# Rebuilding 64-bit weights with a parametric ReLU in an attention and MLP kernel on one core

## The chip, the core and the metric

The kernel runs on one core of a Trainium2 chip. The metric is the device time of one execution in microseconds (us), as the median of several runs. A core has five instruction streams that run side by side and wait for each other through semaphores: TensorE (PE, matrix products into PSUM), VectorE (DVE), ScalarE (ACT), GpSimd (POOL), and SyncE (SP), which here only issues DMA transfers.

## What is computed

```python
q_pool = q.reshape(B, H, S // 2, 2, D).mean(axis=3)         # B, H, S, D = 4, 8, 1152, 64
scores = 1 / sqrt(D) * q_pool @ k.transpose(0, 1, 3, 2)
attn = softmax(scores)
x = (attn @ v), heads side by side                          # 2304 x 512
h = x @ w_in                                                # 512 x 2048
out = (h * sigmoid(h)) @ w_out                              # 2048 x 512, result 2304 x 512
```

The two weight matrices arrive as 64-bit floating point numbers. No engine computes in that format, so the kernel builds the 32-bit number from the two 32-bit words of each weight by integer operations.

## The kernel before

**Attention.** Two heads make a pair, 16 pairs in all, four per batch. A job is one pair and 128 pooled queries; the last 64 queries of two pairs share a job. That gives 18 jobs per batch, 72 in all, numbered from 0. A job computes its scores on PE into the PSUM tiles S0 and S1 (L708), the row maxima on DVE (`TENSOR_REDUCE`, L765), and the exponentials with their sums on ACT (L781, tile p). Each p is split into an fp16 high part (a cast, L398 on ACT or L402 on DVE) and an fp16 remainder (L422, on POOL or DVE), both in the tile phl. Two DMA transposes on SP's queue (L808) turn phl into pt. PE multiplies pt with V (L916, tile po), and DVE divides by the sums (L988, tile x). There is one set of score tiles, so the scores of a job wait for the exponentials of the job before. In the first four jobs one side is transposed by PE (pp, L822) in place of the DMA.

**MLP.** When a batch's four pairs have finished 128 queries, those 512 numbers per row are a block. 18 blocks follow, each of 192 products with w_in (L1111), tanh on ACT (L1125), the gate on DVE (L1132), a split into two fp16 parts (g), and 48 products with w_out (L1206; the last block L1159). PE mixes the blocks' products with the jobs.

**Weights.** `weights(n)` (L540) prepares one of 32 pieces of 128x512 numbers. A transfer brings 128x1024 words into a tile named wide (the first 16 pieces) or raw (the last 16). Then, for each piece:

1. L398 on ACT or L404 on DVE: t = high word, read as fp32, times 2^-111, into a PSUM tile (named mm).
2. L600 on ACT: the top three bits of the low word, in place.
3. L611 on DVE: (t << 3) | low bits. The shift moves exponent and mantissa into their fp32 place and pushes the sign bit out.
4. L619 on DVE: (high word & 0x80000000) | t, which puts the sign back.
5. For w_in alone: a scaling in place (L398).
6. The fp16 high part (L398, ACT) and the fp16 remainder (L422, POOL).

**The order of the work.** `Plan.order` walks through all operations by a priority number and by estimated costs of each engine, and writes one fixed order of instructions per engine. Priorities come from `PRI` (L59) plus the job's number, and from `MLP_EVAC` and `T_EVAC` (L75). An operation with several engines (`either`, L385) goes to the engine that would end it first. With `early=True` DVE is taken off that list. The pools of tiles bound how far the order runs ahead.

Of the kernel before, what the change touches and what calls it, by code (L numbers as in the profile page):

```python
# [27 lines left out]
F32 = mybir.dt.float32  # L28
# [8 lines left out]
P = 128  # L37
# [16 lines left out]
WAIT = 0.206  # L54
PREP_LEAD = 2.029
FIRST_LEAD, FIRST_STEP = -1.602, 3.771
W_FIRST, W_STEP, W2_LATER = 3.378, 0.358, -0.109
V_LATER = 613.5
PRI = dict(  # L59
    score=-3861.412,  # L60
    top=-11.405,
    exp=0.634,
    hi=1.998,
    lo=0.473,
    turn=4.325,
    flip=60509.245,
    flat=-3.873,
    sums=-1535.234,
    rows=-1498.338,
    side=-1.092,  # L70
    load=-8.662,
    raw=0.151,
    xturn=-36.995,
)
EARLY, KL_EARLY, T_EARLY, WLO_EARLY, ADD_EARLY = 8, 2, False, True, True  # L75
MLP_EVAC, T_EVAC = 9.35, -2973.437
# [9 lines left out]
MODE_SWITCH, COLD, COLD_FACTOR = 0.096, 38.0, 2.0  # L86
# [11 lines left out]
EARLY_BY = "act", "dve"  # L98
W_BY = "act", "dve"
# [6 lines left out]
AHEAD, SWITCH, STEAL = 2.802, 386.698, 1.299  # L106
# [18 lines left out]
class Op:  # L125
# [5 lines left out]
    def __init__(self, options, priority, tiles, port, moves, matmuls, mode):  # L131
        self.options, self.priority, self.tiles, self.port = options, priority, tiles, port
        self.moves, self.matmuls, self.mode = moves, matmuls, mode
        self.after, self.before, self.missing = [], [], 0
        self.at = self.start = self.end = None
# [6 lines left out]
class Plan:  # L142
# [7 lines left out]
    def add(self, options, priority, reads=(), writes=(), tiles=(), port=True, moves=None, matmuls=0, mode=0):  # L150
        tiles = [x for t in tiles for x in (t, t.share) if x is not None]
        op = Op(options, priority, tiles, port, moves, matmuls, mode)
# [26 lines left out]
    def order(self):  # L179
# [39 lines left out]

        def pick(e, now):  # L220
            for item in waiting[e]:
                op = item[2]
                if op.at[e] > now + WAIT or not has_room(op):
                    continue
# [23 lines left out]
        while len(order) < len(self.ops):  # L248
# [11 lines left out]
            while moved:  # L260
                moved = False
                for e in engines:
                    if free[e] > now + 1e-9:
                        continue
                    item = pick(e, now)
# [11 lines left out]
                    if e == "pe":  # L277
                        if now < COLD:
                            cost *= COLD_FACTOR
                        if op.mode != mode:  # L280
                            cost += MODE_SWITCH
                        mode = op.mode
# [33 lines left out]
                    order.append(op)  # L316
                    for a in op.after:
# [27 lines left out]
def tile_kernel(tc, q, k, v, w_in, w_out, out):  # L345
    nc = tc.nc
    with ExitStack() as ctx:
# [37 lines left out]
        def either(options, *args, early=False, **kw):  # L385

            if early:  # L390
                options = [o for o in options if o[0] != "dve"] or options
# [909 lines left out]
```

## Time and profile before

| | us |
|---|---|
| median of 3 runs | 723.63 (722.24 to 724.0) |
| the profiled execution's own time | 726.18 |
| its span, from the first to the last instruction | 724.4 |

The span is read as two stretches. In the first 160 us the loads arrive, the weights are rebuilt and the first jobs run. After that, blocks and jobs alternate on PE until only MLP products are left (the last 65 us). The profile has, for each engine, busy times in any stretch; a group's row gives the busy time, the mean duration in nanoseconds and the idle time just before the group's instructions with what ended it; a timeline's row gives start, length, engine, line and operation.

### The profile page before, as it was taken

How to read it: one execution, taken by the hardware profiler on the slowest of the kernel's cores; microseconds unless marked ns; L12 is line 12 of the kernel's file. 1: busy time of each engine (PE TensorE's matmuls, PEld its weight loads, DVE VectorE, ACT ScalarE, POOL GpSimd, SP SyncE). 2: the span in 40 equal slices, each digit the busy share in tenths (PEclk: the TensorE clock that was granted, in tenths of full speed). 3: DMA queues.
4: the chain of work that ended last, by engine and by line, in shares of the span. 5: the costliest groups of instructions: out<-in, count | busy, mean ns of one | idle time of the engine just before them, and what ended most of it. 6: DMA issues, size and time to landing. Idle time of an engine off the chain costs nothing.

```text
span 724.4 us, 23311 instructions
## 1 busy us (share of the span) xinstructions
PE 652.5 (90%) x10052; PEld 470.8 (65%) x10052; DVE 472.4 (65%) x852; ACT 495.6 (68%) x722; POOL 470.7 (65%) x264
## 2 busy tenths in 40 slices
PE   4544877979899999998999999999999999999997
PEld 2333555656758685857585858585758585858767
DVE  3888987977867765775875656477697565754110
ACT  4998897897658676775766767675766675765221
POOL 3536886888657676667647877868547676767111
PEclk8798899999999999999999999999999999999999
DMA  8999889999999999999999999999999998999000
GB/s 345 334 306 216 131 158 226 232 193 206 204 320 189 191 164 179 175 224 184 238 208 198 161 185 165 173 243 191 242 208 182 172 176 160 165 166 161 24 15 16
DMA packets 362888, 138.11 MB, mean 191 GB/s; under 512 B 350112, under 2 KB 350368, under 8 KB 362784
## 3 DMA queue, kind: packets, MB, share of 16 engines
q1 hardware_dynamic: 362624, 136.49, 100.0%
q8 instruction: 78, 1.28, 0.7%
q14 instruction: 26, 0.21, 0.1%
q10 hardware_dynamic: 160, 0.13, 0.1%
HBM read 45.09 MB, written 4.72 MB: 69 GB/s over the span
## 4 chain that ended last, share of the span: by engine, by line
PE 57%; DMA 12%; POOL 9%; DVE 8%; ACT 6%; issue 6%; SPq 1%; POOLq 0%; ACTq 0%; DVEq 0%
PE mm L1111 18%; PE mm L1206 17%; PE S L708 11%; PE po L916 10%; DMA pt<-phl 9%; POOL phl L422 4%; DVE nm L765 4%; POOL w L422 2%; ACT p L781 2%; DMA ld<-v 2%; POOL g L422 2%; ACT phl L398 2%; PE mm L1159 1%; SPq L808 1%; DVE mm L611 1%
## 5 line engine op out<-in xcount | busy, mean ns | idle before, releaser
L422 POOL TENSOR_TENSOR phl<-p,phl 128x1152 f16<-128x1152 f32 x121 | 292.6, 2424 | 125.4 <-ACT phl L398 71.6
L781 ACT ACTIVATE p<-S,nm 128x1152 f32<-128x1152 f32 x144 | 175.0, 1216 | 97.9 <-DVE nm L772 52.1
L765 DVE TENSOR_REDUCE nm<-S 128x1 f32<-128x1152 f32 x144 | 194.6, 1351 | 53.5 <-PE S L708 53.4
L1111 PE MATMUL mm<-xt,w 128*128 128x128 f16 x3456 | 204.4, 220 | 7.0 <-DVE t L1132 4.3
L1111 PEld LDWEIGHTS <-w 128*128 128x128 f16 x3456 | 196.7, 98 | 12.4 <-issue 7.4
L1206 PE MATMUL mm<-w,g 128*128 128x512 f16 x816 | 186.5, 379 | 2.0 <-DVE t L1132 1.4
L916 PE MATMUL po<-V,pt 128*128 128x64 f16 (+1 forms) x4320 | 132.0, 195 | 24.5 <-DMA pt<-phl 12.7
L708 PE MATMUL S<-K,Q 64*128 64x512 f16 (+7 forms) x1320 | 136.3, 369 | 13.7 <-ACT p L781 7.3
L916 PEld LDWEIGHTS <-pt 128*128 128x128 f16 (+1 forms) x4320 | 123.1, 101 | 37.9 <-DMA pt<-phl 16.0
L422 POOL TENSOR_TENSOR g<-t,g 128x512 f16<-128x512 f32 x72 | 96.1, 1337 | 69.6 <-ACT g L398 67.9
L398 ACT ACTIVATE phl<-p 128x1152 f16<-128x1152 f32 x115 | 132.2, 1160 | 9.1 <-DMA pt<-phl 5.9
L1206 PEld LDWEIGHTS <-g 128*128 128x128 f16 x816 | 75.8, 98 | 86.1 <-issue 2.6
L1132 DVE SCALAR_TENSOR_TENSOR t<-t,mm 128x512 f32<-128x512 f32 x72 | 49.4, 686 | 68.8 <-ACT t L1125 68.1
L708 PEld LDWEIGHTS <-Q 64*128 64x128 f16 (+1 forms) x1080 | 42.0, 96 | 50.1 <-issue 9.3
L398 ACT ACTIVATE g<-t 128x512 f16<-128x512 f32 x72 | 45.2, 627 | 21.9 <-DVE t L1132 21.6
L1125 ACT ACTIVATE t<-mm 128x512 f32<-128x512 f32 x72 | 42.5, 590 | 25.4 <-PE mm L1111 25.1
L743 DVE TENSOR_SCALAR r<-sum 128x1 f32<-128x1 f32 (+1 forms) x152 | 17.2, 148 | 52.2 <-ACT p L781 51.7
L708 PEld LDWEIGHTS S<-K,Q 64*128 64x128 f32 (+1 forms) x240 | 22.3, 204 | 39.5 <-issue 22.9
L988 DVE TENSOR_TENSOR x<-po,r 128x128 f32<-128x128 f32 x72 | 20.7, 287 | 21.0 <-PE po L916 18.6
L422 POOL TENSOR_TENSOR xs<-x,xs 128x512 f16<-128x512 f32 (+1 forms) x18 | 22.5, 1248 | 16.6 <-ACT xs L398 16.5
L422 DVE TENSOR_TENSOR phl<-p,phl 128x1152 f16<-128x1152 f32 x19 | 28.3, 1495 | 5.8 <-ACT phl L398 4.9
L525 DVE SCALAR_TENSOR_TENSOR V<-ld,V 128x1152 f16<-128x1152 f32 x16 | 21.9, 1373 | 13.5 <-ACT V L398 13.4
(53 smaller groups left out, 415.2 us busy)
## 6 DMA issues: line engine op xcount, KB each, us to landing
ld<-q SPq DMA_DIRECT2D x16, 576.0 KB, 5.2
ld<-v SPq DMA_DIRECT2D x16, 576.0 KB, 6.1
ld<-k SPq DMA_DIRECT2D x12, 576.0 KB, 6.6
pt<-phl SPq DMA_TRANSPOSE x280, 4.4
wide<-w_in SPq DMA_DIRECT2D x8, 512.0 KB, 7.3
wide<-w_out SPq DMA_DIRECT2D x8, 512.0 KB, 8.1
raw<-w_in SPq DMA_DIRECT2D x8, 512.0 KB, 5.8
raw<-w_out SPq DMA_DIRECT2D x8, 512.0 KB, 5.4
```

The lines of the kernel that those rows point to most:

```text
L398: nc.scalar.activation(out=out(), in_=src(), func=AF.Copy, scale=scale or 1.0)
L422: return lambda: getattr(engine, op)(out=out(), in0=a(), in1=b())
L525: lambda: nc.vector.scalar_tensor_tensor(out=values(1), in0=v3(), scalar=V_SCALE, in1=values(0)[:, :, :D], op0=ALU.mult, op1=ALU.subtract,),
L708: nc.tensor.matmul(o[to, c], lhsT=a[rows, s], rhs=x[rows, c], start=n == 0, stop=n == len(terms) - 1,)
L765: lambda: nc.vector.tensor_reduce(out=nm(), in_=ps()[:, :S], op=ALU.max, axis=AX.X),
L781: lambda: nc.scalar.activation(out=p32(), in_=ps()[:, :S], func=AF.Exp, scale=0.0625, bias=nm(), **({} if SUM_BY_PE else dict(accum_out=sm ...
L916: nc.tensor.matmul(o[to, keep : keep + n], lhsT=pt[:, hl * NK + c, cols], rhs=vv[:, at : at + n], start=c == 0 and hl + vl == 0, stop=c == ...
L988: lambda: nc.vector.tensor_tensor(out=to(), in0=sides2()[:, :, :D], in1=r().unsqueeze(2).to_broadcast([P, 2, D]), op=ALU.mult,),
L1111: nc.tensor.matmul(o, lhsT=w[:, f // 2 % 4, wl, cols], rhs=moving(xl, kk), start=kk == 0 and wl + xl == 0, stop=kk == 3 and wl == 1,)
L1125: lambda: nc.scalar.activation(out=t(), in_=h(), func=AF.Tanh, scale=1.0 / G_SCALE),
L1132: lambda: nc.vector.scalar_tensor_tensor(out=t(), in0=t(), scalar=1.0, in1=h(), op0=ALU.add, op1=ALU.mult,),
L1206: nc.tensor.matmul(o(), lhsT=g[ff // 4]()[:, gl, ff % 4], rhs=w[:, u % 4, wl, e * DM : e * DM + DM], start=ff == ffs[0] and gl + wl == 0, ...
```

## The change

- Steps 1 and 4 of a weight become one. `Prelu` on ACT multiplies by 2^-111, and negative numbers by -(2^32) in addition. A negative weight so leaves step 1 positive, with an exponent larger by 32, which is one bit; the shift by three moves that bit to the sign's place. Step 3 then writes the finished number straight into the tile wide or raw, and L619 is gone. Step 1 can no longer go to DVE.
- Step 2 may go to DVE as a logical shift to the right by 29, step 5 to ACT, DVE or POOL, step 6's cast to ACT, DVE or POOL.
- The flag `early` is gone: in the first jobs the casts and remainders of p, q, k, v and the weights may go to DVE.
- All priorities are new numbers, the first 8 jobs get additions of their own (`PRE`, `SOON`), the weights' steps too (`W`), and the MLP's operations have one number each (`EV`). The planner's notion of when PE's products cost double is a different one. `SPARE` is 0, so no filler product is made.
- The correction of the sums (`guard`) is one instruction with two constants in place of one; the second constant is 1.

```diff
-MLP_EVAC, T_EVAC = 9.35, -2973.437
+PRE = dict(
+    score=-0.266, top=0.223, exp=2.744, hi=1.295, lo=-1.698, turn=-0.57, sums=1.5, side=-0.268,
+)
+W = dict(
+    t=0.374, low=0.166, put=-3777.77, more=0.289, hi=0.49, lo=-0.918,
+)
...
-W_BY = "act", "dve"
+W_BY = "act", "dve", "pool"
+MORE_BY = "act", "dve", "pool"
+LOW_BY = "act", "dve"
...
-            if early:
-                options = [o for o in options if o[0] != "dve"] or options
...
-            either(
-                cast(512, t, value, 2.0**-111, fast=False),
-                pr, [("raw", *tok)], [("t", *tok)], [t, raw], port=False, early=T_EARLY,
-            )
+            add(
+                "act", act_cost(512, True) + 0.06,
+                lambda: nc.scalar.activation(
+                    out=t(), in_=value(), func=AF.Prelu, scale=2.0**-111, alpha=-(2.0**32)
+                ),
+                pr + W["t"], [("raw", *tok)], [("t", *tok)], [t, raw], port=False,
+            )
...
+            def low_on(engine):
+                return lambda: engine.tensor_scalar(
+                    out=words(0).bitcast(U32), in0=words(0).bitcast(U32), scalar1=29, scalar2=None,
+                    op0=ALU.logical_shift_right,
+                )
...
             add(
                 "dve", slow,
                 lambda: nc.vector.scalar_tensor_tensor(
-                    out=tu(), in0=tu(), scalar=3, in1=words(0).bitcast(U32),
+                    out=words(1).bitcast(U32), in0=tu(), scalar=3, in1=words(0).bitcast(U32),
                     op0=ALU.logical_shift_left, op1=ALU.bitwise_or,
                 ),
-                T_EVAC, [("low", *tok)], [("t", *tok)], [t, raw], port=False,
-            )
-            add(
-                "dve", slow,
-                lambda: nc.vector.scalar_tensor_tensor(
-                    out=words(1).bitcast(U32), in0=words(1).bitcast(U32), scalar=0x80000000,
-                    in1=tu(), op0=ALU.bitwise_and, op1=ALU.bitwise_or,
-                ),
-                T_EVAC, [("t", *tok)], [("raw", *tok)], [t, raw], port=False,
+                pr + W["put"], [("low", *tok), ("t", *tok)], [("raw", *tok)], [t, raw], port=False,
             )
```

**The order on DVE at the start.** S are the scores of job 0, V the split values, ld a loaded tile. Before:

```order
L525 SCALAR_TENSOR_TENSOR V_117<-ld_91,V_117 128x1152
L765 TENSOR_REDUCE nm_126<-S_14_110 128x1
L772 TENSOR_SCALAR nm_126<-nm_126 128x1
L765 TENSOR_REDUCE nm_133<-S_13_109 128x1
L772 TENSOR_SCALAR nm_133<-nm_133 128x1
L525 SCALAR_TENSOR_TENSOR V_128<-ld_97,V_128 128x1152
```

Now (line numbers shift by 10 to 19):

```order
L432 TENSOR_TENSOR Q_103<-ld_87 128x576
L535 SCALAR_TENSOR_TENSOR V_117<-ld_91,V_117 128x1152
L432 TENSOR_TENSOR Q_122<-ld_93 128x576
L784 TENSOR_REDUCE nm_125<-S_14_110 128x1
L791 TENSOR_SCALAR nm_125<-nm_125 128x1
L784 TENSOR_REDUCE nm_132<-S_13_109 128x1
L791 TENSOR_SCALAR nm_132<-nm_132 128x1
L535 SCALAR_TENSOR_TENSOR V_127<-ld_97,V_127 128x1152
```

The additions that pool q for jobs 0 and 1 came from POOL to DVE, and the second of them stands ahead of job 0's maxima.

**The order on ACT at the first weights.** wide_107 holds the first four pieces, mm is the PSUM tile t, pt and pp belong to job 0. Before:

```order
L398 ACTIVATE mm_178<-wide_107 128x512
L600 ACTIVATE wide_107<-wide_107 128x512
L398 ACTIVATE mm_184<-wide_107 128x512
L600 ACTIVATE wide_107<-wide_107 128x512 x2
L398 ACTIVATE wide_107<-wide_107 128x512
L672 ACTIVATE pt_157<-pp_191 128x128
L398 ACTIVATE w_0_39_197<-wide_107 128x512
```

Now (L606 is the Prelu, L613 the low bits):

```order
L613 ACTIVATE wide_107<-wide_107 128x512
L606 ACTIVATE mm_180<-wide_107 128x512
L613 ACTIVATE wide_107<-wide_107 128x512
L606 ACTIVATE mm_184<-wide_107 128x512
L408 ACTIVATE wide_107<-wide_107 128x512
L408 ACTIVATE w_0_37_191<-wide_107 128x512
```

The two pieces follow each other with the same kinds of steps; L619 between the merge and the scaling is what is missing on DVE.

**The order on SP at the loads of pair 3.** ld and K are the loads of q, k and v, wide those of weights. Before:

```order
L585 DMA wide_107<-w_in 128x1024 x2
L585 DMA wide_107<-w_out 128x1024
L464 DMA ld_124<-q 128x1152
L464 DMA K_130<-k 128x1152
L464 DMA ld_140<-v 128x1152
```

Now:

```order
L595 DMA wide_107<-w_in 128x1024 x2
L595 DMA wide_107<-w_out 128x1024 x2
L595 DMA wide_129<-w_in 128x1024 x2
L595 DMA wide_129<-w_out 128x1024
L827 DMA_TRANSPOSE pt_175<-phl_161 128x9x128 x2
L474 DMA ld_201<-q 128x1152
L474 DMA K_204<-k 128x1152
L474 DMA ld_215<-v 128x1152
```

The loads of pair 3 moved behind four more loads of weights and behind the first two transposes.

## Rows read from the trace of the kernel before

**Rows 1.** The page: the span

```profile
span 724.4 us, 23311 instructions
```

**Rows 2.** Windows: length, PE, PEld, DVE, ACT, POOL busy us, then PEclk, DMA, GB/s

```profile
0.00:160.00 160.00, 105.48 (x1292) 72.20 (x1292) 125.84 (x228) 133.24 (x206) 106.06 (x71) 0.90 1.00 240
20.00:80.00 60.00, 32.65 (x368) 21.70 (x365) 51.09 (x92) 55.85 (x92) 31.69 (x22) 0.83 1.00 265
80.00:160.00 80.00, 63.63 (x898) 45.39 (x897) 67.42 (x126) 68.42 (x104) 65.50 (x41) 0.98 1.02 193
160.00:724.00 564.00, 546.99 (x8764) 398.61 (x8761) 346.59 (x625) 362.41 (x517) 364.67 (x194) 1.00 1.01 177
```

**Rows 3.** Timeline of PE: start, length; scores of jobs 0, 3, 8 and 18

```profile
6.10 4.21 PE L708 MATMUL S<-K,Q 64*128 64x512 f32 x12 [6.10 <-POOL Q L422]
...
40.34 2.21 PE L708 MATMUL S<-K,Q 64*128 64x512 f32 x12 [0.27 <-issue]
...
92.71 2.21 PE L708 MATMUL S<-K,Q 64*128 64x512 f32 x12 [1.46 <-ACT p L781]
...
183.71 1.64 PE L708 MATMUL S<-K,Q 64*128 64x512 f16 x18
```

**Rows 4.** Waits of PE from 160 us on: total us, times, longest

```profile
PE po L916 <- DMA pt<-phl: 11.2, 13, 2.1
```

**Rows 5.** Timeline of ACT: steps from one start to the next

```profile
67.42 1.15 ACT L398 ACTIVATE phl<-p 128x1152 f16<-128x1152 f32 x1
68.47 0.65 ACT L600 ACTIVATE wide<-wide 128x512 int32<-128x512 uint16 x1
...
70.77 1.21 ACT L600 ACTIVATE wide<-wide 128x512 int32<-128x512 uint16 x2
71.87 1.21 ACT L781 ACTIVATE p<-S,nm 128x1152 f32<-128x1152 f32 x1
```

**Rows 6.** Groups by form: the weights' operations | busy, mean ns | idle before

```profile
L619 DVE SCALAR_TENSOR_TENSOR wide<-wide,mm 128x512 uint32<-128x512 uint32 x16 | 11.0, 689 | 0.7
L611 DVE SCALAR_TENSOR_TENSOR mm<-mm,wide 128x512 uint32<-128x512 uint32 x16 | 11.1, 697 | 2.8 <-ACT wide L600 1.4 <-ACT mm L398 0.9
L404 DVE TENSOR_SCALAR mm<-wide 128x512 f32<-128x512 f32 x9 | 6.2, 686 | 0.1
L398 ACT ACTIVATE mm<-wide 128x512 f32<-128x512 f32 x7 | 4.4, 627 | 0.9 <-DMA wide<-w_in 0.9
L600 ACT ACTIVATE wide<-wide 128x512 int32<-128x512 uint16 x16 | 10.4, 666 | 0.5 <-DMA wide<-w_in 0.5
```

**Rows 7.** Timeline of DVE: the first job, and the step of the second merge

```profile
9.52 1.36 DVE L525 SCALAR_TENSOR_TENSOR V<-ld,V 128x1152 f16<-128x1152 f32 x1 [9.52 <-ACT V L398]
10.80 1.35 DVE L765 TENSOR_REDUCE nm<-S 128x1 f32<-128x1152 f32 x1
...
65.39 0.69 DVE L619 SCALAR_TENSOR_TENSOR wide<-wide,mm 128x512 uint32<-128x512 uint32 x1
66.00 1.35 DVE L765 TENSOR_REDUCE nm<-S 128x1 f32<-128x1152 f32 x1
```

**Rows 8.** Groups by form: nearest rows to the operations that are new

```profile
L402 DVE CAST phl<-p 128x1152 f16<-128x1152 f32 x25 | 19.7, 789 | 1.6 <-issue 0.9 <-DMA pt<-phl 0.3
L422 DVE TENSOR_TENSOR ld<-ld 128x576 f32<-128x576 f32 x9 | 10.7, 1192 | 0.8 <-DMA ld<-q 0.7
L1125 ACT ACTIVATE t<-mm 128x512 f32<-128x512 f32 x72 | 42.5, 590 | 25.4 <-PE mm L1111 25.1
```

**Rows 9.** Timeline of SP's queue, and the page's DMA issues: KB, us to landing

```profile
19.18 9.36 SPq L808 DMA_TRANSPOSE pt<-phl  x2
...
ld<-k SPq DMA_DIRECT2D x12, 576.0 KB, 6.6
```

**Rows 10.** Timeline of POOL: the same addition without and with DVE's V work beside it

```profile
4.60 1.40 POOL L422 TENSOR_TENSOR Q<-ld 128x576 f32<-128x576 f32 x1 [3.23 <-DMA ld<-q]
9.81 2.33 POOL L422 TENSOR_TENSOR Q<-ld 128x576 f32<-128x576 f32 x1 [3.81 <-DMA ld<-q]
```

More of the change, by code (lines that the diff above doesn't have):

```diff
@@ L105 @@
 LAST = B * FULL + B // 2 - 1
-AHEAD, SWITCH, STEAL = 2.802, 386.698, 1.299
 class Tile:
@@ L218, in departs, with windows @@
             return now
+        warm, used, busy, until = False, 0.0, 0.0, WINDOW
+        def windows(now):
+            nonlocal warm, used, until
+            while now >= until:
+                warm = used >= (COOL if warm else HOT) * WINDOW
+                used = min(WINDOW, max(0.0, busy - until))
+                until += WINDOW
         def pick(e, now):
@@ L222, in pick @@
                 op = item[2]
+                if op.spare and warm and used > KEEP * WINDOW:
+                    continue
                 if op.at[e] > now + WAIT or not has_room(op):
@@ L247, in order @@
                 release(op, 0.0)
-        while len(order) < len(self.ops):
+        todo = sum(not op.spare for op in self.ops)
+        while todo:
             if not events:
@@ L277, in order @@
                     if e == "pe":
-                        if now < COLD:
-                            cost *= COLD_FACTOR
+                        if not warm:
+                            cost *= 2.0
                         if op.mode != mode:
                             cost += MODE_SWITCH
-                        mode = op.mode
+                        mode, busy = op.mode, now + cost
+                        used += min(busy, until) - now
                     op.start, op.end = now, now + cost
@@ L533, in prepare @@
                     "pool", 0.1, lambda: nc.gpsimd.memset(values(0)[:, :, D : D + 1], 1.0),
-                    pr + V_LATER, [], [("one", p)], [vt[p]],
+                    pr + (V_FIRST if first else V_LATER), [], [("one", p)], [vt[p]],
                 )
@@ L603, in shift @@
                 )
+            def low_on(engine):
[3 more added lines that the diff above has]
+                )
+            ways = {
+                "act": ("act", act_cost(512) + 0.02, low_act),
+                "dve": ("dve", dve_cost(512, True), low_on(nc.vector)),
+            }
             either(
-                [("act", act_cost(512), shift)],
-                pr, writes=[("low", *tok)], reads=[("raw", *tok)], tiles=[raw], port=False,
+                [ways[x] for x in LOW_BY],
+                pr + W["low"], writes=[("low", *tok)], reads=[("raw", *tok)], tiles=[raw],
             )
@@ L630, in weights @@
                 either(
-                    cast(512, value, value, more, by=W_BY),
-                    pr, writes=[("raw", *tok)], tiles=[raw], early=True,
+                    [(e, c + (0.15 if e == "act" else 0.0), f) for e, c, f in cast(512, value, value, more, by=MORE_BY)],
+                    pr + W["more"], writes=[("raw", *tok)], tiles=[raw],
                 )
@@ L728, in job @@
             add(
-                "pe", cost, lambda: scores(j), j + PRI["score"],
+                "pe", cost, lambda: scores(j), j + pri(j, "score"),
                 inputs, [("S", j, 0), ("S", j, 1)], [*st["S"], *own],
@@ L1127, in first @@
                     ),
-                    MLP_EVAC, [], [tok, ("gt", bid, u)], [h, t], port=False,
+                    EV["tanh"], [], [tok, ("gt", bid, u)], [h, t], port=False,
                 )
@@ L1247, in block, with spin, matmuls @@
             second()
+        def spin(n):
+            ps = tile("psM", "mm", [P, 512], F32, "spin")
+            def matmuls():
+                x = one().bitcast(F16)
+                for _ in range(4):
+                    nc.tensor.matmul(ps()[:, :256], lhsT=x[:, :P], rhs=x, start=True, stop=True)
+            add("pe", 4 * pe_cost(256), matmuls, 1e8 + n, [("one",)], [], [ps, one], matmuls=4, spare=True)
+        for n in range(SPARE):
+            spin(n)
         for p in range(PPB):
```

128 lines of the change are left out of this document (63 added, 65 removed).

## The prediction

> **What bounds the kernel now.** I read the busy times by stretch first, because the kernel has two stages with different limits [rows 2]. From 160 us to the end PE is busy 547.0 of 564 us at the full granted clock: that stage is as long as its products. In the first 160 us PE is busy 105.5 us, so 54.5 us of its 71.5 idle us lie there, and the granted clock is 0.90 on average, 0.83 between 20 and 80 us, a mixture of 1.2 and 2.4 GHz. There ACT is busy 55.9 of 60 us and DVE 51.1, POOL only 31.7. Between 80 and 160 us ACT, DVE and POOL all have 65 to 68 of 80 us. So the start is paced by ACT, with DVE close behind, and whatever shortens ACT's and DVE's work per job in the start moves the whole PE-bound stage forward. The scores show the pace [rows 3]: job 0 at 6.1 us, job 8 at 92.7, job 18 at 183.7.
>
> After 160 us the 17 us of idle PE are mostly waits of the products with V for their transposes, 11.2 us in 13 waits [rows 4].
>
> **What the change does on ACT.** I counted instructions in the two orders up to the same landmark, the exponentials of a job, and priced each by the step from one start to the next, since ACT's instructions overlap a little: 1.05 us for a cast of 1152 columns and 0.55 us for one of 512 [rows 5]. Up to job 8: low bits 22 to 10, -6.6 us; casts of p 12 to 9, -3.2; copies for t 7, now 19 Prelus, +6.6 if a Prelu takes a copy's time; scalings 10 to 8, -1.1; high casts of weights 19 to 15, -2.2; other 512-wide ones five to three, -1.1. Sum -7.6 us. Up to job 12 the same counting gives -11.3 us, up to job 17 -7.9 us, since by then all 32 Prelus stand against 10 copies.
>
> The price of the Prelu is in no row. Its bounds: from below the tanh of 512 columns out of PSUM, 590 ns [rows 8]; from above twice the copy into PSUM, 1254 ns. I take the copy itself, 627 ns [rows 6], since it has the same operands and a tanh costs no more than a copy. The Trainium skill, on the page "ScalarE: Activation LUTs", section "Step-by-step: what each stage is for", states one element per cycle and lane whatever the function. By that the Prelu costs what the copy does, which is the sum above; no row here shows a Prelu. The order has a single load of activation tables, as before, so no switch of tables is added.
>
> **What it does on DVE.** Up to the maxima of job 8 it loses 19 second merges, whose step is 0.61 us [rows 7], and 12 copies of 686 ns [rows 6]: -19.8 us. It gains 11 shifts, three casts of p at 0.79 us and two additions of q at 1.19 us [rows 8], and four operations of 512 columns, for which I take the merge's 0.69 [rows 6]. A shift of 512 columns in place lies between 0.35 us, the cast's rate [rows 8] on fewer columns, and 0.69 us, the rate of the merges; I take 0.40, since like the cast it has one source and lies in SBUF. That adds 4.4 + 2.4 + 2.4 + 2.8 = 12.0 us, or 15.2 with slow shifts. Sum -7.8 us, or -4.6. So both engines that pace the start are relieved by nearly the same amount, and neither hides the other's gain. The merge that stays writes SBUF from PSUM and SBUF, as the removed one did, so I leave it at 0.69 us. The correction of the sums keeps its count and size: nothing. The new maker of filler products is switched off: nothing.
>
> **What it moves.** On DVE the second addition of q stands ahead of job 0's maxima. V's remainder ran 9.52 to 10.88 us and the maxima began at 10.80 [rows 7]; they now wait one addition more, +1.2 us, which the queue behind them (V of pair 1, the sums) and ACT's first exponentials inherit. On SP the loads of pair 3 come behind four more loads of weights and two transposes. Before, those transposes held the queue from 19.2 to 28.5 us [rows 9]; the loads then land some 6 us later [rows 9], near 34 us, while job 3's scores started at 40.3 [rows 3], and would start near 37 now. I cost this at nothing; the cover is about 3 us, and what comes later than that delays job 3 by as much. The transposes of job 0 are queued ahead of them and need POOL's remainder.
>
> **The sum.** What counts is how much PE work is done by when. From the scores of job 56 on PE's order is the same in both. Ahead of job 8's scores the new order has 1.3 us more products (24 L1111 fewer, 12 L1206 more), ahead of job 12's 3.3 us less, ahead of job 18's 4.2 us more. The gain on ACT plus that, less the 1.2 us: 7.7 at job 8, 6.8 at job 12, 7.9 + 4.2 - 1.2 = 10.9 at job 18. PE is saturated between the last two, nearer to the last. I take 9.5 us. In the PE-bound stage I expect no change: DVE, ACT and POOL have 61 to 65% there, and the loads of the later batches stand within one job of where they stood in SP's order. 724.4 us [rows 1] become 714.9. The profiled execution took 726.18 us, 2.6 above the median of 723.63, and its span 0.8 above it; I take the gain from the median: 723.63 - 9.5 = **714.1 us**.
>
> The spread of this case: slow shifts would make DVE the bound and leave 4.6 - 1.2 + 1.3, some 5 us; the end at job 18 gives 11. Scores at the low clock take 4.21 us where warm ones take 2.21 [rows 3]; a job or two more or fewer in that state are 2 to 4 us. The waits for transposes [rows 4] can move by a third, 4 us. Together 707 to 720.
>
> **The rivals.**
> - *The removed work was covered.* POOL and the transposes, not ACT and DVE, would pace the stretch from 80 to 160 us, and the gain up to job 8 is given back there. For it: POOL is busy 65.5 of 80 us there [rows 2]; and the same addition of q took POOL 1.40 us with DVE idle and 2.33 us beside DVE's V work with two SBUF inputs [rows 10, 7]. The change puts 13 shifts and eight more casts of p on DVE up to job 17, 13 x 0.40 + 8 x 0.79 = 11.5 us in which POOL might stand. Against it: POOL has 14.5 idle us there and half of 20 to 80 us. If two thirds of the 11.5 us fell on the path, 1.8 us of gain would be left: 721.8. The Trainium skill, "GPSIMD Engine Reference", "Key points", says that GpSimd shares its SBUF interfaces with VectorE and contends with VectorE's two-port modes or two SBUF inputs. That speaks against this change; the rows on the addition agree for two inputs, and no row here shows it for a one-source operation.
> - *Prelu is dear.* On ACT, behind each Prelu the scalings, casts and exponentials wait. If it goes through the columns twice, each costs 0.43 us more (a cast of 1152 columns takes 0.50 us more than one of 512 [rows 5], 0.78 ns a column, times 512 gives 0.40; the upper bound above gives 0.63; I take 0.43, a little over the first). At 0.43, 32 of them are 13.8 us: 714.1 + 13.8 = 727.9, slower than before. It decides from 9.5 / 32 = 0.30 us on, a Prelu of 0.93 us. Against it: tanh, exponential and copies all keep one rate.
> - *More is gained.* PE, with fewer holes, keeps 2.4 GHz through the start, and the new priorities close half of the waits after 160 us: 9.5 + 3 + 5.6, 705.5 us. For it: clock 0.83 between 20 and 80 us. Against it: the places of the loads and transposes in SP's order hardly moved.
> - *The new order waits more in the middle.* The waits of rows 4 double: 714.1 + 11.2 = 725.3.
>
> **How the numbers follow.** The forecast has 0.62, covered work 0.13, more gain 0.12, the dear Prelu 0.06, more waits 0.07. The range for 8 in 10 takes the forecast's spread and most of the larger gain and of the covered case: 706 to 722. About 0.3%, 2.2 us, is what a measurement of this kernel can tell from no change. Faster by more than that, below 721.4: the forecast, the larger gain and nearly half of the covered case, 0.79. Within it: the rest of the covered case and some of the waits, 0.11. Slower: 0.10.
>
> **What would show it.** Right: job 8's scores near 85 us and job 18's near 176; busy DVE in the first 160 us lower by some 10 us at equal work; Prelus of 0.6 to 0.7 us; PE's idle time from 160 us on about 17 us as before. Shifts near 0.4 us show the DVE price, additions of q ahead of job 0's maxima the 1.2 us. Wrong: Prelus above 0.9 us; POOL over 95% busy from 80 to 150 us, with its remainders longer than now; job 3 waiting for its loads; or waits for transposes well over 11 us.

## The result, and the profile after

| kernel | median us | lowest to highest | runs |
|---|---|---|---|
| before | 723.71 | 722.24 to 724.0 | 4 |
| changed | 715.92 | 714.45 to 718.18 | 4 |
| changed, in the next series | 714.53 | 711.05 to 715.39 | 6 |

The ratio of changed to before is 0.9897, with a 95% interval of 0.9872 to 0.9921: 1.0% faster, 7.8 us by the medians. The second series gave 0.9868 [0.9846, 0.9890] against a median of 722.89 us of the kernel before. The forecast was 714.1 us. The profiled execution of the changed kernel took 714.45 us, the lowest of its four, and that of the kernel before 726.18, above the highest of the table; so their spans differ by more, 11.9 us, than the medians. A second profile of the changed kernel (714.33 us) has job 8's and job 18's scores within 1 us of the first, so what is read below from the pair of traces is some 3 to 4 us more than the medians bear out, and most of that belongs to the one execution of the kernel before.

The page of the changed kernel, its span and PE's line:

```profile
span 712.5 us, 23295 instructions
...
PE 653.3 (92%) x10052; PEld 470.7 (66%) x10052; DVE 471.9 (66%) x839; ACT 480.4 (67%) x707; POOL 463.9 (65%) x260
```

Windows of the changed kernel (busy us with the number of instructions in brackets, then granted clock, DMA share, GB/s). They answer to [rows 2]:

```profile
core 0: us, PE busy (x) PEld busy (x) DVE busy (x) ACT busy (x) POOL busy (x), PEclk, DMA share, GB/s
0.00:160.00 160.00, 116.32 (x1456) 79.47 (x1458) 120.48 (x221) 132.03 (x209) 112.20 (x76) 0.90 1.05 251
20.00:80.00 60.00, 38.88 (x482) 26.71 (x479) 49.56 (x94) 52.21 (x86) 41.94 (x29) 0.82 1.00 270
80.00:160.00 80.00, 67.61 (x948) 47.45 (x949) 59.83 (x113) 69.47 (x111) 65.80 (x40) 0.98 1.11 210
160.00:712.00 552.00, 537.03 (x8600) 391.20 (x8596) 351.46 (x619) 348.36 (x499) 351.65 (x185) 1.00 0.99 178
```

PE's idle time in the first 160 us fell from 54.5 to 43.7 us, and after 160 us from 17.0 to 15.0. So 10.8 of the 12.8 us that PE idles less lie in the start, at an unchanged granted clock of 0.90. DVE and ACT were not busier; they did less for each job. The products themselves took the same time in both, 652.5 us busy before and 653.3 now over the whole span, so all of the gain is idle time of PE.

The scores of jobs 3, 8 and 18 in PE's timeline answer to [rows 3]: 3.5, 8.3 and 5.3 us earlier.

```profile
36.87 2.21 PE L723 MATMUL S<-K,Q 64*128 64x512 f32 x12 [0.27 <-issue]
...
84.41 2.21 PE L723 MATMUL S<-K,Q 64*128 64x512 f32 x12
...
178.43 1.64 PE L723 MATMUL S<-K,Q 64*128 64x512 f16 x18
```

How much work each engine did up to the same scores is read from windows that end where these start. The kernel before, to jobs 8, 12 and 18:

```profile
0.00:92.71 92.71, 50.01 (x533) 33.54 (x533) 70.11 (x125) 73.57 (x116) 49.94 (x36) 0.85 0.97 265
0.00:133.85 133.85, 84.42 (x999) 58.61 (x999) 104.13 (x187) 108.32 (x170) 83.42 (x57) 0.89 0.98 242
0.00:183.71 183.71, 129.19 (x1641) 87.64 (x1642) 143.58 (x260) 152.13 (x232) 124.60 (x81) 0.92 1.02 233
```

The changed kernel, to the same jobs:

```profile
0.00:84.41 84.41, 51.39 (x520) 33.09 (x520) 64.44 (x116) 66.87 (x106) 50.81 (x39) 0.84 0.97 283
0.00:122.48 122.48, 79.53 (x957) 54.06 (x957) 90.94 (x165) 96.60 (x153) 80.12 (x56) 0.89 1.02 261
0.00:178.43 178.43, 134.14 (x1743) 90.94 (x1744) 137.15 (x246) 144.92 (x227) 126.59 (x83) 0.91 1.05 247
```

ACT has 6.7, 11.7 and 7.2 us less to do (predicted 7.6, 11.3 and 7.9), DVE 5.7 us less to job 8 (predicted 7.8). PE's work moved by +1.4, -4.9 and +5.0 us (predicted +1.3, -3.3, +4.2).

The groups of the weights' steps (busy us, mean ns, idle time before) answer to [rows 6]; L606 is the Prelu, L613 and L619 the low bits on ACT and on DVE, L634 the merge that stays:

```profile
L606 ACT ACTIVATE mm<-raw 128x512 f32<-128x512 f32 x16 | 9.9, 626 | 0.3 <-DVE x L1007 0.3
L606 ACT ACTIVATE mm<-wide 128x512 f32<-128x512 f32 x16 | 9.8, 631 | 0.0
L613 ACT ACTIVATE raw<-raw 128x512 int32<-128x512 uint16 x11 | 7.1, 663 | 3.6 <-DMA raw<-w_in 3.6
...
L619 DVE TENSOR_SCALAR raw<-raw 128x512 uint32<-128x512 uint32 x5 | 5.5, 1114 | 0.0
L619 DVE TENSOR_SCALAR wide<-wide 128x512 uint32<-128x512 uint32 x8 | 3.7, 482 | 0.2 <-DMA wide<-w_out 0.2
...
L634 DVE SCALAR_TENSOR_TENSOR wide<-mm,wide 128x512 uint32<-128x512 uint32 x16 | 10.6, 685 | 3.4 <-ACT mm L606 3.4
```

The Prelu costs what the copy did, 627 ns. The shift was expected at 0.40 us; 13 of them took 9.2 us together, 0.71 each, because some of them waited for POOL (the last section has the rows).

### The profile page after: what moved, and what is told of

Its sections match the earlier page's. It is cut to its first block, busy times and chain, and to the rows that moved or that the text cites. A ratio compares the mean times of both kernels' runs of the same rounds, so it can differ in the third digit from the quotient of the medians.

```text
span 712.5 us, 23295 instructions
## 1 busy us (share of the span) xinstructions
PE 653.3 (92%) x10052; PEld 470.7 (66%) x10052; DVE 471.9 (66%) x839; ACT 480.4 (67%) x707; POOL 463.9 (65%) x260
## 5 line engine op out<-in xcount | busy, mean ns | idle before, releaser
L432 POOL TENSOR_TENSOR g<-t,g 128x512 f16<-128x512 f32 x72 | 98.4, 1368 | 80.4 <-ACT g L408 79.6
L723 PE MATMUL S<-K,Q 64*128 64x512 f16 (+7 forms) x1320 | 138.2, 373 | 13.4 <-ACT p L800 6.7
L408 ACT ACTIVATE phl<-p 128x1152 f16<-128x1152 f32 x99 | 114.4, 1160 | 8.2 <-DMA pt<-phl 5.8
L412 DVE CAST phl<-p 128x1152 f16<-128x1152 f32 x41 | 33.7, 822 | 9.9 <-DMA pt<-phl 7.1
L432 POOL TENSOR_TENSOR xs<-x,xs 128x512 f16<-128x512 f32 (+1 forms) x16 | 19.8, 1238 | 24.3 <-ACT xs L408 24.1
L432 DVE TENSOR_TENSOR phl<-p,phl 128x1152 f16<-128x1152 f32 x21 | 32.1, 1533 | 4.4 <-ACT phl L408 4.2
L535 DVE SCALAR_TENSOR_TENSOR V<-ld,V 128x1152 f16<-128x1152 f32 x16 | 27.6, 1729 | 6.6 <-ACT V L408 6.6
```

The source lines that it names most:

```text
L408: nc.scalar.activation(out=out(), in_=src(), func=AF.Copy, scale=scale or 1.0)
L412: nc.vector.tensor_copy(out=out(), in_=src())
L432: return lambda: getattr(engine, op)(out=out(), in0=a(), in1=b())
L535: lambda: nc.vector.scalar_tensor_tensor(out=values(1), in0=v3(), scalar=V_SCALE, in1=values(0)[:, :, :D], op0=ALU.mult, op1=ALU.subtract,),
L723: nc.tensor.matmul(o[to, c], lhsT=a[rows, s], rhs=x[rows, c], start=n == 0, stop=n == len(terms) - 1,)
```

## The experiments

Eleven kernels besides the changed one were run. Two things were kept apart: which operations are issued, and in which order. Where an edit reaches the planner, a new order is written for the whole kernel; "in place" means that the order was kept and only the instruction at its place was exchanged. Each run's ratio is told against the kernel before on the same chip (medians 722.57 to 723.47 us); differences to the changed kernel are taken from its second series, 714.53 us.

The theory: ACT and DVE both pace the start, and the change pays because it takes work from both. The rivals: the work removed was covered; or the order, not the operations, makes the gain.

### The changed kernel again, and one engine's work put back (in place)

The changed kernel without an edit:

> The changed kernel unchanged, timed again beside the others of this call. Both theories: ratio to before 0.987 to 0.992 (714 to 718 us), job 8's scores near 84 us, job 18's near 178 us; a reference for the other runs of this call.

Measured 714.53 us. The second merge put back in place, with a plain copy for the Prelu:

```diff
-                lambda: nc.scalar.activation(
-                    out=t(), in_=value(), func=AF.Prelu, scale=2.0**-111, alpha=-(2.0**32)
-                ),
+                lambda: nc.scalar.activation(out=t(), in_=value(), func=AF.Copy, scale=2.0**-111),
...
+                nc.vector.scalar_tensor_tensor(
+                    out=words(1).bitcast(U32), in0=words(1).bitcast(U32), scalar=0x80000000,
+                    in1=tu(), op0=ALU.bitwise_and, op1=ALU.bitwise_or,
+                )
...
```

> The changed kernel with the second merge put back on DVE right behind the first (32 instructions of 0.69 us, a step of 0.61, 19.5 us in all, 11.6 us up to job 8), t by a plain copy on ACT, every other instruction in the changed kernel's order. Theory (DVE and ACT pace the first 160 us, so a DVE step there costs time): most of the gain is lost, 8 to 13 us slower than the changed kernel, 724 to 729 us. Rival (the removed merge was covered and the gain comes from the new order, priorities and engine choices): within 3 us of the changed kernel, 714 to 719 us.

Measured 726.17 us, ratio 1.0037 [1.0018, 1.0057], 11.6 us above the changed kernel. Each Prelu issued twice in place:

```diff
-                lambda: nc.scalar.activation(
+                lambda: [nc.scalar.activation(
                     out=t(), in_=value(), func=AF.Prelu, scale=2.0**-111, alpha=-(2.0**32)
-                ),
+                ) for _ in range(2)],
```

> The changed kernel with every Prelu issued twice on ACT (32 more instructions at a step of 0.55 us, 17.6 us in all, 10.5 us up to job 8), every other instruction in the same order. Theory (ACT paces the start): 9 to 15 us slower than the changed kernel, 725 to 731 us, job 8's scores near 94 us. Rival (POOL, the transposes or the job's chain of waits pace the start, ACT has room): 0 to 4 us slower, 716 to 720 us.

Measured 722.79 us, 0.9992 [0.9974, 1.0010], 8.3 us above the changed kernel. The first 160 us, with the merge back (first row) and with Prelus doubled (second):

```profile
0.00:160.00 160.00, 109.53 (x1290) 74.32 (x1290) 127.91 (x231) 124.31 (x194) 101.18 (x69) 0.89 0.99 238
```

```profile
0.00:160.00 160.00, 108.91 (x1316) 72.50 (x1316) 110.83 (x207) 142.12 (x227) 103.41 (x71) 0.89 1.00 239
```

Now DVE (127.91 us) or ACT (142.12) is the busiest, the other falls back, and PE gets 109 us of work done in place of 116.32. So neither engine has slack for 32 more instructions: 32 merges at a step of 0.61 us are 19.5 us, of which 11.6 / 19.5 = 0.59 fell on the path; 32 Prelus at 0.55 are 17.6, of which 8.3 / 17.6 = 0.47 did. "Covered work" falls in this order.

These two prices hold more than waiting. The same runs up to job 18's scores, with the merge back (first row) and with Prelus doubled (second), have the same products ahead of them as the changed kernel's window that ends at 178.43:

```profile
0.00:190.08 190.08, 137.97 (x1742) 94.39 (x1743) 154.57 (x278) 148.35 (x227) 125.32 (x83) 0.91 1.01 233
```

```profile
0.00:187.81 187.81, 134.33 (x1744) 90.71 (x1744) 134.26 (x246) 165.45 (x259) 125.57 (x83) 0.91 1.02 237
```

PE idles 52.1 and 53.5 us there against 44.3, that is 7.8 and 9.2 us more; with the merge back it is also busy 3.8 us longer for the same products. That run's granted clock was 0.94 from 80 to 160 us, against 0.98. By idle time alone the merges cost 0.40 us per us and the Prelus 0.52, so which of the two engines is the tighter one is not settled by the two prices.

### The operations alone, in the old order

The first try let the planner write the order. The kernel before, with Prelu and one merge:

```diff
-            either(
-                cast(512, t, value, 2.0**-111, fast=False),
+            add(
+                "act", act_cost(512, True) + 0.06,
+                lambda: nc.scalar.activation(
+                    out=t(), in_=value(), func=AF.Prelu, scale=2.0**-111, alpha=-(2.0**32)
+                ),
...
```

> The kernel before with the Prelu and the single merge alone; old priorities, low bits on ACT alone, casts of the first jobs barred from DVE as before. DVE loses 32 merges and 22 copies, ACT gains 22 Prelus of 0.55 us (12 us). Theory (ACT paces the start, DVE is close behind): without DVE taking shifts and casts, ACT gets longer, so little is gained or something lost: 720 to 728 us. Rival (the removed merge alone makes the gain): 713 to 718 us.

Measured 754.62 us, 1.0434 [1.0414, 1.0453]: far outside what either theory expected. Between 60 and 100 us:

```profile
60.00:100.00 40.00, 10.74 (x32) 4.53 (x31) 17.18 (x26) 37.35 (x61) 24.61 (x18) 0.59 0.44 114
```

```profile
PE S L703 <- ACT p L776: 29.3, 2, 19.1
```

In ACT's order 16 and then 17 steps of weights stand in a row ahead of two exponentials, and the scores wait 29.3 us for these. V of pair 3 was split behind the same steps. One number of the change was added, the early priority of V's split in the first batch:

```diff
-                pr + V_LATER, [("ld", p, "v")], [("vh", p)], [vt[p], tv], early=first,
+                pr + (-45.048 if first else V_LATER), [("ld", p, "v")], [("vh", p)], [vt[p], tv], early=first,
...
```

> The kernel before with Prelu and one merge (the run that took 754.6) and one number more of the change: V's cast and remainder of the first batch get the priority -45.0 in place of +613.5. In that run V of pair 3 was split behind 33 weight steps on ACT, the products with it could not run, and the tiles of jobs 5 and 6 stayed held. Theory (the place of V's split made the loss, through the tiles): the stop between 60 and 100 us is gone, 718 to 735. Rival (ACT is simply overloaded by 32 Prelus with the bars on DVE in force): 745 or more.

Measured 749.92 us, 1.0367 [1.0331, 1.0404]. The time is the rival's, the stop is gone: PE is busy 29.12 us between 60 and 100 us again, against 27.11 in the kernel before. What the run loses instead is mostly clock: in its profile PE's 10052 products take 669.3 us in place of 652.5, at a mean granted clock of 0.957 against 0.978, and PE idles 9.5 us more. So it does not show that ACT was overloaded. With the planner in between, the operations could not be judged. So the kernel before was changed in place: the same instructions at the same places, each copy (on ACT or DVE) now a Prelu on ACT, the second merge left out.

```diff
...
-                cast(512, t, value, 2.0**-111, fast=False),
+                [(e, c, prelu) for e, c, _ in cast(512, t, value, 2.0**-111, fast=False)],
...
-                    out=tu(), in0=tu(), scalar=3, in1=words(0).bitcast(U32),
+                    out=words(1).bitcast(U32), in0=tu(), scalar=3, in1=words(0).bitcast(U32),
...
-                lambda: nc.vector.scalar_tensor_tensor(
-                    out=words(1).bitcast(U32), in0=words(1).bitcast(U32), scalar=0x80000000,
-                    in1=tu(), op0=ALU.bitwise_and, op1=ALU.bitwise_or,
-                ),
+                lambda: None,
```

> The kernel before in its own order, place by place: each copy for t, on ACT or DVE, becomes a Prelu on ACT at the same place of the program, the first merge writes the finished number and the second is not issued. Nothing is planned anew, all priorities, the bar and the low bits on ACT stay. Up to job 8 DVE loses 19 merges (11.6 us) and 12 copies (8.2 us), ACT gains 12 steps of 0.55 us (6.6 us). Theory (the operations taken away make the gain, and what the earlier runs of Prelu alone lost was the order that the planner then wrote): by the prices so far, 0.59 us per us of DVE and 0.47 per us of ACT, -11.7 + 3.1, about 714, 710 to 718. Rival (with 32 Prelus ACT is the bound unless DVE and POOL take other work from it): 721 or more.

Measured 724.24 us, 1.0022 [1.0001, 1.0043]: no gain. From 20 to 160 us, the kernel before, this one, and the changed kernel:

```profile
20.00:160.00 140.00, 96.28 (x1266) 67.10 (x1262) 118.51 (x217) 124.27 (x195) 97.19 (x62) 0.91 1.01 224
```

```profile
20.00:160.00 140.00, 100.63 (x1284) 68.55 (x1282) 82.81 (x165) 134.56 (x218) 97.77 (x62) 0.88 0.98 223
```

```profile
20.00:160.00 140.00, 106.48 (x1430) 74.16 (x1428) 109.39 (x206) 121.69 (x196) 107.74 (x68) 0.91 1.07 236
```

DVE lost 36 of its 118.5 us and ACT rose to 134.56 of 140. DVE's waits in the first 160 us (us in total, times, longest) say whom it now waits for:

```profile
engine line waited for: us in total, times, longest us
DVE raw L616 <- ACT mm L595: 12.6, 9, 2.9
DVE V L525 <- ACT V L398: 10.5, 2, 9.1
DVE wide L616 <- ACT mm L595: 9.6, 8, 2.0
```

The merges wait 22.2 us for Prelus. In the changed kernel DVE has 26.6 us more and ACT 12.9 less than here. So in the old order the Prelu does not pay by itself, and ACT, now the busiest, is the likely reason.

The traces show one thing beside that. Up to job 18's scores the old order has the same products, and the window is

```profile
0.00:182.25 182.25, 131.94 (x1640) 87.71 (x1641) 107.63 (x206) 161.91 (x254) 124.92 (x81) 0.89 1.00 235
```

PE idles 4.2 us less than in the kernel before (50.3 against 54.5), but is busy 2.75 us longer for the same products, at a granted clock of 0.89 against 0.92. This profiled execution, 721.52 us, is the lowest of its twelve, so a gain of some us in idle time is not shown by it.

The change also hands other work of ACT to DVE. That hand-over was tried in the old order too: the run above with all 32 low bits as shifts on DVE, in place.

```diff
-                nc.scalar.activation(
-                    out=words(0).bitcast(I32), in_=halves(1).bitcast(U16), func=AF.Copy,
-                    scale=2.0**-13, bias=2.0**-14 - 0.5,
+                nc.vector.tensor_scalar(
+                    out=words(0).bitcast(U32), in0=words(0).bitcast(U32), scalar1=29, scalar2=None,
+                    op0=ALU.logical_shift_right,
```

> The run of Prelu and one merge in the order of the kernel before (724.2, no gain, ACT busy 18 to 20 of every 20 us from 20 to 160 us, DVE 11 to 14) with all 32 low bits issued as shifts on DVE at the same places. Up to job 8 ACT loses 22 steps of 0.55 us, 12.1 us, and DVE gains 22 shifts of 0.43 to 1.11 us, 9 to 24 us, about what it had lost. Theory (the merge's removal pays once ACT hands as much work to DVE as the Prelus bring it): at 0.47 us per us of ACT 5.7 us less, 715 to 720. Rival (the old order itself stands in the way, only the new priorities turn the freed time into a gain): 722 or more.

Measured 731.95 us, 1.0140 [1.0100, 1.0180]: the theory falls, and the time is the rival's. Up to job 18's scores:

```profile
0.00:187.30 187.30, 134.03 (x1641) 90.58 (x1642) 133.38 (x236) 146.29 (x222) 127.51 (x81) 0.89 0.97 227
```

For the same products as in the kernel before, DVE has 10.2 us less to do and ACT 5.8 less, and PE still comes to job 18 3.6 us later. PE idles only 1.3 us less (53.3 against 54.5) and is busy 4.8 us longer, at a granted clock of 0.89 against 0.92. Over the whole span PE's products take 659.5 us against 652.5 and PE idles 74.7 against 71.9, so 7.0 of the 9.8 us between the two traces are products that took longer. A part of the relief went into waiting: the shifts stand on DVE where ACT had its low bits, and ACT's exponentials now wait for row maxima behind them.

```profile
ACT p L783 <- DVE nm L774: 8.7, 8, 3.2
```

In the kernel before, exponentials waited 0.3 us for maxima in the first 160 us. The shifts themselves waited for POOL too: 32 of them took 30.1 us, against 13.4 at the 0.42 us of one alone. So relief of both engines is not enough by itself. Whether the place of the steps on their queues, the shifts' waits or the clock made the difference to the changed kernel was not separated.

### Parts of the change undone in the new order

The bar restored that keeps DVE from the first jobs' casts and remainders and the weights' (planned anew):

```diff
-        def either(options, *args, **kw):
+        def either(options, *args, early=False, **kw):
+            if early:
+                options = [o for o in options if o[0] != "dve"] or options
...
-                    pr + W["more"], writes=[("raw", *tok)], tiles=[raw],
+                    pr + W["more"], writes=[("raw", *tok)], tiles=[raw], early=True,
...
-                at + pri(j, "hi"), [("p32", j, i)], [("phi", j, i)], [p32, phl],
+                at + pri(j, "hi"), [("p32", j, i)], [("phi", j, i)], [p32, phl], early=j < 8,
...
```

> The changed kernel with the bar restored that keeps DVE away from the casts and remainders of the first jobs and from the weights' scalings, casts and remainders; the order is planned anew. ACT's order then has 15 weight steps in a row ahead of the second exponential of job 4. Theory (the freedom of engines is needed because 32 Prelus now stand on ACT): DVE gives work of the first 8 jobs to ACT and POOL, job 8 comes 8 us or more later, 722 to 735. Rival (the merge's removal does it all, the bar is indifferent): 712 to 717.

Measured 735.57 us, 1.0182 [1.0139, 1.0224], just above the theory's range. PE's longest new wait in the start is a product with V. Its PSUM tile comes from the same two buffers as a weight's t, and t is held until the merge that reads it:

```profile
PE po L937 <- DVE raw L636: 14.1, 4, 10.3
```

The changed kernel with all numbers of the kernel before:

```diff
-WAIT = 0.189
+WAIT = 0.206
...
-    score=-258.189, top=-1.612, exp=-1.381, hi=1.631, lo=-0.034, turn=5.489, flip=13904.244,
+    score=-3861.412, top=-11.405, exp=0.634, hi=1.998, lo=0.473, turn=4.325, flip=60509.245,
...
```

> The changed kernel (Prelu, one merge, free engines, its planner) with all priorities and switches of the kernel before: no own priorities for the first 8 jobs, for the weights' steps or for the MLP's operations. Theory (operations taken away make the gain, the numbers only trim it): 714 to 721. Rival (the new priorities carry a good part of the gain themselves): 722 or more, no faster than the kernel before.

Measured 729.37 us, 1.0091 [1.0059, 1.0123]: the rival holds, and by more than it expected. The start is not where it falls behind: PE is busy 116.16 us in the first 160, as in the changed kernel (116.32). But it lost the clock on the way:

```profile
80.00:160.00 80.00, 66.88 (x894) 46.16 (x896) 63.14 (x114) 67.00 (x110) 57.88 (x35) 0.91 1.00 195
```

The granted clock is 0.91 in that stretch against 0.98, so part of its products ran at 1.2 in place of 2.4 GHz, and as many busy us held fewer of them. Its page has over the whole span

```profile
PE 661.4 (91%) x10052; PEld 475.3 (65%) x10052; DVE 454.6 (63%) x820; ACT 494.4 (68%) x724; POOL 466.5 (64%) x262
```

against 653.3 us for the same number of products in the changed kernel. Of the 14.1 us between the two spans, 8.1 are thus products that took longer, and 6.0 are idle time of PE, all of it after 160 us.

The low bits on ACT alone, first planned anew, then in place:

```diff
-LOW_BY = "act", "dve"
+LOW_BY = ("act",)
```

> The changed kernel with the low bits (step 2) on ACT alone, as in the kernel before; the order is planned anew. 13 shifts leave DVE (8 on wide at 0.48 us, 5 on raw at 1.11 us, 9.4 us) and come to ACT as steps of 0.55 us, 7.2 us. Theory (DVE and ACT both pace the start; added DVE time cost 0.59 us per us and added ACT time 0.47 in the runs so far): -5.6 + 3.4, within 3 us of the changed kernel's 714.5, 711 to 718. Rival (ACT alone paces the start, the shifts on DVE are what the change lives from): 7.2 us on the path or a little less, 720 to 723.

```diff
-                "dve": ("dve", dve_cost(512, True), low_on(nc.vector)),
+                "dve": ("dve", dve_cost(512, True), low_act),
```

> The changed kernel in its own order, place by place, with the 13 shifts on DVE issued as low bits on ACT at the same place of the program. DVE loses 9.4 us (8 at 0.48, 5 at 1.11), ACT gains 13 steps of 0.55, 7.2 us. Theory (both pace the start, at the prices so far): -5.5 + 3.4, about 712, 709 to 716. Rival 1 (ACT alone is the bound): 717 to 722. Rival 2 (the earlier run with low bits on ACT alone, 735.6, was right, and ACT cannot carry them in any order): 725 or more.

Measured 735.58 us (1.0181 [1.0143, 1.0220]) when planned anew, above all that was expected, and 717.94 us (0.9924 [0.9894, 0.9954]) in place. The same 13 exchanges cost 21.0 us in one order and 3.4 in the other (2.0 against the changed kernel's first series), so some 17.6 us of the first were the planner's new order and not ACT's work. It had, for one, waits of PE for transposes in the start that the changed kernel has for 2.0 us only:

```profile
PE po L935 <- DMA pt<-phl: 11.5, 4, 6.1
```

The one in place missed the theory's range and lies at the low end of the first rival: if ACT's 7.2 us cost what 0.47 us per us makes, 3.4, then DVE's relief of 9.4 us earned nothing; the run does not tell the two apart.

### A version with less work

Step 5 scales w_in in place because it is kept at 2^4 times its value, while step 1 leaves 2^8. Kept at 2^8, it needs no step 5; tanh and the output divide by the larger factor. In place, the 16 scalings are not issued:

```diff
-W_IN_SCALE = 2.0**4
+W_IN_SCALE = 2.0**8
...
-                    [(e, c + (0.15 if e == "act" else 0.0), f) for e, c, f in cast(512, value, value, more, by=MORE_BY)],
+                    [(e, c + (0.15 if e == "act" else 0.0), lambda: None) for e, c, f in cast(512, value, value, more, by=MORE_BY)],
```

> The changed kernel in its own order, place by place, with the 16 scalings in place of w_in (step 5) not issued: w_in is kept 2^8 times its value, as w_out is, in place of 2^4 times, and tanh and the output take the other factor out. 13 of them are ACT's (0.55 us a step, 7.2 us in all) and 3 POOL's. Theory (ACT is still on the path in the changed kernel): 0.47 x 7.2 = 3.4 us less than the changed kernel's 714.5, 711, 707 to 713. Rival (the start is now paced by DVE, POOL or the transposes, ACT's steps are covered): 713.5 to 716.

Measured 716.57 us, 0.9898 [0.9866, 0.9929]: the rival holds, no gain over the changed kernel (0.9868 and 0.9897 in its two series).

```profile
0.00:160.00 160.00, 114.37 (x1382) 78.28 (x1383) 118.64 (x215) 121.14 (x189) 105.68 (x71) 0.89 1.06 249
```

ACT has 11 us less in the first 160 us (121.14 against 132.03), DVE and PE about the same. PE idles 45.6 us there against 43.7, and 60.7 against 59.2 over the whole span, so the clock does not hide a gain. Adding to either engine costs, taking from ACT alone earned nothing: that fits two engines that hand work to each other in turn, where the slower one at each place counts, but no run shows this hand-over place by place. No version beat the changed kernel.

## Why the prediction was right, and where not

- **What bounds the start: right in the two engines.** Work put back on DVE costs 0.59 us per us, on ACT 0.47. That "whatever shortens ACT's and DVE's work per job in the start" moves the rest forward is too wide: less work on ACT alone (716.57 us), and less on both in the old order (731.95), moved nothing forward.
- **"Both engines ... are relieved by nearly the same amount, and neither hides the other's gain": right**, and this carried the forecast. Relief of 6.7 us (ACT) and 5.7 (DVE) up to job 8 went with 8.3 us; in the old order relief of DVE with more work on ACT gave nothing over the kernel before (724.24 us), relief of ACT alone nothing over the changed one (716.57). Counting only the removed operation, without what moved to DVE, would have missed it. That ACT's relief counts at its full length, as the sum has it, no run shows: at the prices of the two runs above, 6.7 x 0.47 + 5.7 x 0.59 make 6.5 us. Some 0.7 us of the 8.3 come from V's load, which landed earlier in that execution, so the closeness at this point is partly luck.
- **The Prelu's price: right**, 626 and 631 ns against 627 taken. The dear Prelu, and with it the rival on the slower side, falls.
- **The shift's price: right for a shift alone (0.42 us against 0.40), wrong for the shifts as they ran.** They took 0.71 us in the mean, slightly above the upper bound of 0.69, because five of the 13 waited for POOL; the prediction put this wait at nothing. 11 shifts at 0.31 more are 3.4 us, and 7.8 - 3.4 = 4.4 is near the bound of 4.6 that the prediction kept; 5.7 was measured. For slow shifts the prediction named "some 5 us" in all; the medians gained 7.8 and 8.4.
- **The 1.2 us for the addition of q: wrong.** DVE's timeline answers to [rows 7]:

```profile
8.79 1.36 DVE L535 SCALAR_TENSOR_TENSOR V<-ld,V 128x1152 f16<-128x1152 f32 x1 [3.28 <-ACT V L408]
10.07 0.75 DVE L432 TENSOR_TENSOR Q<-ld 128x576 f32<-128x576 f32 x1
10.74 1.35 DVE L784 TENSOR_REDUCE nm<-S 128x1 f32<-128x1152 f32 x1
```

  V's remainder began 0.73 us earlier and the addition took 0.75, not the 1.19 of [rows 8], which is a mean with POOL beside it. The maxima began at 10.74 against 10.80, but that is luck of the one execution: V's load landed earlier in it. From the start of V's cast on ACT to the maxima it is 3.14 us now against 2.47 before, so the addition costs 0.67 us. Every run that kept the changed kernel's order has these 3.14 us, and V's cast began between 7.34 and 8.27 us in them.
- **The loads behind weights and transposes: right.** The two transposes kept SP's queue from 16.97 to 25.58 us, pair 3's q was issued at 25.63, and job 3's scores began at 36.87 without a wait for a load; 37 was expected.
- **The sum: nearly right.** Up to job 18 it said 10.9 us; the scores came 5.3 us earlier with 5.0 us more products ahead of them, 10.3. (They began at 178.4 us; near 176 was named, where its own 7.9 less 1.2 makes 177.) The forecast took 9.5, and 7.8 and 8.4 were measured in the medians of two series, so the forecast lies 1 to 2 us above the medians and the pair of traces above both.
- **The PE-bound stage: no change was predicted**, 2.0 us less idle time was found in one profile. The waits for transposes fell from 11.2 us [rows 4] to 7.8, others came in:

```profile
PE po L935 <- DMA pt<-phl: 7.8, 13, 1.9
PE mm L1130 <- DMA xt<-xs: 1.8, 1, 1.8
```

- **The rivals.** Covered work by POOL falls: POOL is busy 56.0 of the 70 us from 80 to 150, 80%, where over 95% was its sign, though its remainders of p grew from 2383 to 2452 ns in the first 160 us. The larger gain falls: the clock from 20 to 80 us stayed, 0.82 against 0.83. More waits in the middle fall: those of [rows 4] shrank from 11.2 to 7.8 us. One sign of being right did not come: DVE's busy time in the first 160 us fell by 5.4 us and not by some 10, though with 10.8 us more of PE's work done in them.
- **What the prediction could not show** is that the gain hangs on the whole order. It read the order as given and summed over it, and for that order the sum holds. The in-place runs in the old order (724.24, 731.95) and the newly planned ones (729.37 to 754.62) show that the Prelu with one merge gains nothing, or loses up to 32 us, in another order. With the merge back in the new order (726.17) and the Prelu in the old one (724.24) neither half pays alone. What limits the start once ACT is relieved further (716.57) stays open, and so does whether a better order exists.

## What to carry to other kernels

When two engines share the path, cost a change on both, in the order that will run: less work on ACT alone was worth nothing here, and so was less on DVE with more on ACT. Where a planner writes the order, change the instruction in place to learn what an operation costs, and plan anew only to learn what the planner does with it; here the same 13 exchanges cost 3.4 us in the one case and 21.0 in the other. Busy totals find the engines that pace a stage, but they do not tell how long a new order takes: one with less for both engines to do than the kernel before was 9 us slower than it. Compare them up to the same job and not over a fixed stretch, and split what PE lost into idle time and products that took longer: in three of the runs here the second was the larger part.

## What was not expected of the hardware

One-source operations on DVE were held up by POOL as whole instructions. A shift alone took 0.42 us; of the pair at 38.82 us the second began at 39.17, behind POOL's instruction, and took 2.59 us. The two rows of DVE and the one of POOL beside the pair:

```profile
28.77 0.42 DVE L619 TENSOR_SCALAR wide<-wide 128x512 uint32<-128x512 uint32 x1
...
38.82 2.94 DVE L619 TENSOR_SCALAR raw<-raw 128x512 uint32<-128x512 uint32 x2
```

```profile
38.92 2.55 POOL L432 TENSOR_TENSOR phl<-p,phl 128x1152 f16<-128x1152 f32 x1
```

POOL's remainder ended at 41.47 us and the shift at 41.76, 0.29 later: it waited for the end of POOL's instruction. All 45 shifts of the changed kernel's trace and of the run with 32 on DVE fit that: the 19 that began with no POOL instruction running took 0.41 to 0.43 us, and 25 of the 26 that began during one ended 0.28 or 0.29 us after it (the other, at its very end, 0.35). Casts of p on DVE did the same in these two traces: 0.74 to 0.76 us without, and those that took longer ended 0.61 or 0.62 us after POOL's instruction. In the run with 32 shifts on DVE they took 0.71 us (on wide) and 1.21 us (on raw) in the mean, 30.1 us together:

```profile
L605 DVE TENSOR_SCALAR raw<-raw 128x512 uint32<-128x512 uint32 x16 | 19.0, 1212 | 0.0
...
L605 DVE TENSOR_SCALAR wide<-wide 128x512 uint32<-128x512 uint32 x16 | 11.1, 708 | 0.0
```

The merge, which reads one operand from PSUM, kept 684 to 699 ns in the mean in the kernel before, the changed one and the in-place runs, most of its instances beside a POOL instruction. The Trainium skill, "SBUF — State Buffer", section "Who interferes with whom", says that DVE's tensor_scalar in a mode with two ports and POOL lock a pair of ports for a whole instruction, the later one waits, and that a DVE instruction with one SBUF input outside such modes does not contend. The rows of the shift and of the merge agree with both halves. So a one-source operation in SBUF moved to DVE beside a busy POOL is to be priced with what is left of POOL's instruction, not with its own length alone.
